# Windowed attention with a feed-forward layer: a refitted planner and a new order of the same work

## The chip, the core and the metric

The kernel runs on one core of a Trainium2 chip. The engines that compute are TensorE (PE: matmuls; PEld is its weight load), VectorE (DVE), ScalarE (ACT) and GpSimd (POOL); SyncE (SP) only issues DMAs. The metric is the device time of one execution in microseconds (us). Before the change the median of 8 runs is 217.38 us, from 216.2 to 218.05.

## What is computed

Attention over 4 batches of 8 heads with 768 positions and 64 values per head; each position sees itself and the 95 before it, and the first 8 positions of its batch ("global"), with a bias by distance. Its output, as 3072 rows of 512, goes through a feed-forward layer: 512 to 2048, h - tanh(h), 2048 to 512.

```python
scores = scale * np.matmul(q, k.transpose(0, 1, 3, 2))
rel = pos[:, None] - pos[None, :]
is_global = pos[None, :] < n_global            # 8
is_local = (rel >= 0) & (rel < n_local)        # 96
dist = np.where(is_global & ~is_local, float(n_local), np.abs(rel))
scores = np.where(is_global | is_local, scores - slopes * dist, -1e9)
a = softmax(scores)
x = (a @ v).transpose(0, 2, 1, 3).reshape(3072, 512)
h = x @ w_in
out = (h - np.tanh(h)) @ w_out
```

## The kernel before

The 3072 rows are 24 tiles of 128, numbered u; six tiles make a batch. A tile's query window reaches into its own 128 keys (o=0) and the 128 before (o=1). Every piece of work has a name, and these names are used from here on:

- `ld kf/qf/vf u` (L211, L216): k, q and v of tile u. The first two tiles' k and q come in fp32 by SP and ACT and are cast (`ck`, `cq`, L238); all else is loaded and cast to bf16 by POOL's DMA queue. `in j`, `out j` (L229): eighths of the two weights, on the same queue.
- `T1 u`, `T u` (L247): for tiles 0 to 7 k and q are transposed on TensorE (L258 with 128 columns, L262 in halves), and `Te u` (L270, L277) copies them out of PSUM. From tile 8 on (`PE_T`) one DMA transpose issued by SP does it (`a_DT`, L264, tile qk).
- `B u` (L282, L149): the bias, put into PSUM by a matmul ahead of the scores, for tiles 0 to 2; `mk` (L156, L149) makes, by the same matmul, the masks that later tiles are multiplied by. Both need the tile dT, which is made on DVE (`distance`, L122) from an iota on POOL and eight scaled identities (`slope`, L142).
- `S u` (L287, L295): scores, transposed; `E u o` (L300): exp on ACT; `M u o` (L305): mask on DVE; `AV u` (L313, L319 and L323): times v, with a row of ones for the sums; `R u` (L327): reciprocal and scaling on DVE, which gives x.
- `X u`, `Xe u` (L342, L354): x transposed on TensorE and copied, for tiles 0 to 8 (`PE_X`); from tile 9 on `Xe u` is a DMA transpose issued by SP (`a_DX`, L357, L358).
- `m1 g f` (L371, L377): x @ w_in for a group g: tiles 0 to 5 singly, then groups of three (m1 7 takes tiles 9, 10 and 11). `th` (L386) and `g` (L390) are tanh on ACT and the subtraction on DVE. `m2 u n` (L402, L409): g @ w_out; `ev` (L414, L419) copies the result out of PSUM and `store` (L421) sends it. The last tile is done in column parts (`parts`, L399).

Nothing here loops in the usual sense. A planner, run when the program is built (`plan`, L585), keeps a model of when each engine, each PSUM bank, each buffer and two DMA rings come free, takes at each step the piece of work that could start earliest, and so writes down one order for each engine. The costs are constants: `op(..., us, ...)` for engines, `T_...` for DMAs, `SLACK_DT` and `SLACK_DX` for how much later than modelled a DMA transpose is assumed to land, `ring` and `share` for the DMA rings, `LOADS` (L433) for the order of the first loads (t: a tile's k, q and v; i: an eighth of w_in; o: of w_out). `NUDGE` shifts the priority of single pieces of work. Each engine then runs its list strictly in order and waits on semaphores; a piece of work whose input is late holds all that stands behind it on that engine.

`with_warm` (L716) fills TensorE's list, up to 14 us of the planner's time, with matmuls of zeros into an unused PSUM bank (`warm`, L368) wherever the plan has a hole. DVE's list begins with the memsets of `ident`, `zero` and eleven tiles of ones (L735 to L738); POOL's with one memset, the identity (L110) and the iotas (L117).

Of the kernel before, what the change touches and what calls it, by code (L numbers as in the profile page):

```python
# [8 lines left out]
BF16 = mybir.dt.bfloat16  # L9
# [6 lines left out]
def kernel(  # L16
# [11 lines left out]
    nc = tc.nc  # L28

    B, H, S, Dh = q.shape  # L30
    P = 128
    NQ = S // P
    NP = H // 2
    NU = B * NQ
# [5 lines left out]
    DM = moe_w_in.shape[0]  # L40
# [10 lines left out]
    PLAIN = 2  # L51
# [14 lines left out]
    cpool = ctx.enter_context(tc.tile_pool(name="const", bufs=1))  # L66
# [17 lines left out]
    slopes = cpool.tile([P, H, P], BF16, name="slopes")  # L84
    xT0 = cpool.tile([P, CD, N0 * P], BF16, name="xT0")
    g0 = cpool.tile([P, CF, N0 * P], BF16, name="g0")
    zero = cpool.tile([P, 512], BF16, name="zero")
    NB = 8
    ps = ps_pool.tile([P, NB, 512], FP32, name="ps")
    banks = {}  # L90
# [75 lines left out]
    ops = {}  # L166
    w_in_r = moe_w_in.rearrange("(c p) f -> p c f", p=P)
    w_out_r = moe_w_out.rearrange("(c p) d -> p c d", p=P)
    PE, ACT, DVE, POOL, SP = ENG.PE, ENG.Activation, ENG.DVE, ENG.Pool, ENG.SP
# [26 lines left out]
    kf, qf, vf = {}, {}, {}  # L196
    kq = {}
# [13 lines left out]
    def load_plain(u, nm):  # L211
        src, dst, eng = {"kf": (k, kf, nc.sync), "qf": (q, qf, nc.scalar)}[nm]
        dst[u] = stpool.tile([P, 2, TJ * Dh], FP32, name=nm)
        started(("ld", nm, u), eng.dma_start(out=dst[u], in_=rows_of(src, u)))
# [151 lines left out]
        return b, i * P, n, 512 // n  # L366

    def warm():  # L368
        nc.tensor.matmul(ps[:, NB - 1, :], zero[:, 0:P], zero, start=True, stop=True)  # L369

    def m1(g, f0):  # L371
        b, o, n, m = shape1(g)
# [24 lines left out]
        )  # L397

    def parts(u):  # L399
        return [(0, 256), (256, 384), (384, 512)] if u == NU - 1 else [(0, DM)]  # L400

    def m2(u, n):  # L402
        part, qq = divmod(n, 4)
# [22 lines left out]

    AHEAD = 5.5
    INF = 1.0e9
    NUDGE = {}
    SLACK_DT, SLACK_DX = 5.0, 2.0  # L430
    WARM = (1.3, 14.0)
    T_ROWS, T_LD, T_W, T_ST, T_DT, T_DX = 0.66, 0.95, 1.32, 0.7, 1.75, 0.9
    LOADS = "tttiiiitiitoooiootiooot"  # L433
    first, n_of = [], {"t": 0, "i": 0, "o": 0}
    for c in LOADS + "t" * NU:
        if n_of[c] < (NU if c == "t" else WJ):
# [12 lines left out]
    for it in first:  # L449
        if it[0] != "t":  # L450
            load(it, 0.75, lambda it=it: load_w(it), T_W)
            continue
        u = it[1]
        for nm in ("vf", "kf", "qf") if u == 0 else ("kf", "qf", "vf"):
            key = ("ld", nm, u)
            if u < PLAIN and nm != "vf":
                op(key, SP, 0.0, lambda: None, at={"kf": (4.75, 7.0), "qf": (4.05, 5.45)}[nm][u], pri=-3,
                   take=["kq"] if nm == "kf" else [])
                continue
            after = []  # L460
            if nm == "vf" and u >= NV:
                after += [("AV", u - NV + 1), ("V", (u - NV) // NQ * NQ + NQ - 2)]
            rows = u < ROWS and nm != "vf"
            load(key, 0.7 if rows else 0.88, lambda u=u, nm=nm: load_bf(u, nm), T_ROWS if rows else T_LD,
                 after=after, take=["kq"] if nm == "kf" else [], slack=1.0 if u == PLAIN + 1 else 0.15)

    op(("dT", 0), DVE, 1.2, distance_0, after=[("nums",)], pri=-2)
    op(("dT", 1), DVE, 0.6, distance_1, after=[("nums",), ("issue", ("dT", 0))], pri=-1)
# [10 lines left out]
    for g, us in enumerate(groups):  # L479
        b, o, n, m = shape1(g)  # L480
# [4 lines left out]
    for m in range(3):  # L485
        for a in range(2):
# [3 lines left out]
               free=[("mk", m, a)], pri=1)  # L490

    for u in range(NU):
# [8 lines left out]
        if u < PE_T:  # L501
            t_us = 0.47 if PLAIN <= u < ROWS else 0.24
            apart = u < APART
            for j, r in ((1, rk), (0, rq)):
                prior = [("issue", ("T1", u))] if j == 0 else []
                name = ("T1" if j else "T", u)
# [3 lines left out]
                     lambda eng, u=u, j=j: a_Te(u, j, eng),  # L510
                     after=[("T1" if j and apart else "T", u)] + ([] if apart or j else [("Te", u, 1)]),
                     free=[name] if apart else [] if j else [("T1", u)])
# [5 lines left out]
        if u < BIASED:  # L518
            for o in os:
                op(("B", u, o), PE, 0.44, lambda u=u, o=o: a_B(u, o), pri=1,  # L520
                   after=biased_by + [("dT", 1) if o else None,
                                    ("issue", ("B", u, 0) if o else ("S", u - 1, 0)) if u or o else None],
                   hold=[(("S", u, o), 2)])
                op(("S", u, o), PE, 0.43, lambda u=u, o=o: a_S(u, (o,)),
                   after=te + [("B", u, o), kdep if o else None])
        else:
            op(("S", u, 0), PE, 0.65 if i else 0.43, lambda u=u, os=os: a_S(u, os),
               after=te + [kdep], hold=[(("S", u, o), 2) for o in os])
        for o in os:
            op(("E", u, o), ACT, 0.93, lambda u=u, o=o: a_E(u, o), after=[("S", u, o if u < BIASED else 0)],  # L530
               take=["p%d" % o], free=[("S", u, o)])
            if u >= BIASED:
                op(("M", u, o), DVE, 0.61, lambda u=u, o=o: a_M(u, o),
                   after=[("E", u, o)] + [("mke", mask_of(u, o), a) for a in range(2)])
        pm = "M" if u >= BIASED else "E"
        if 1 <= i < NQ - 1:
# [3 lines left out]
           after=[(pm, u, 0), (pm, u, 1) if i else None, rv, ("V", u - 1) if i >= 2 else None],  # L540
# [5 lines left out]
        if u < PE_X:  # L546
            op(("X", u), PE, 0.23, lambda u=u: a_X(u), after=[("R", u)], hold=[(("X", u), 1)], give=["x"])
            flex(("Xe", u), [(DVE, 0.34), (ACT, 0.5)], lambda eng, u=u: a_Xe(u, eng),
                 after=[("X", u), xdep], take=xtake, free=[("X", u)])
        else:  # L550
            op(("Xe", u), SP, 0.2, lambda u=u: a_DX(u), after=[("R", u), xdep],
               take=xtake, give=["x"], dma=T_DX, slack=SLACK_DX)
    for g, us in enumerate(groups):
        b, o, n, m = shape1(g)
        w = m * n / 1000.0
        end_b = b and us[-1] % HT == (N0 + HT - 1) % HT
        for f in range(0, CF, m):
            op(("m1", g, f), PE, CD * m * (n / 2400.0 + 0.0025), lambda g=g, f=f: m1(g, f),
               after=[("Xe", us[-1]), ("in", (f + m - 1) // FJ)], hold=[(("m1", g, f), 1)], pri=2,
               give=["xT"] if f + m == CF and end_b else [])  # L560
            op(("th", g, f), ACT, 0.1 + 0.82 * w, lambda g=g, f=f: m1_th(g, f), after=[("m1", g, f)],
               take=["th"], pri=2)
            op(("g", g, f), DVE, 0.06 + 1.05 * w, lambda g=g, f=f: m1_g(g, f), after=[("th", g, f)],
               take=["g"] if f == 0 and b else [], give=["th"], free=[("m1", g, f)], pri=2)
    for u in range(NU):
        g = group_of[u]
        m = shape1(g)[3]
        n_u = 4 * len(parts(u))
        for n in range(n_u):
            part, qq = divmod(n, 4)  # L570
            lo, hi = parts(u)[part]
            op(("m2", u, n), PE, 4 * ((hi - lo) / 2400.0 + 0.0025), lambda u=u, n=n: m2(u, n),
               after=[("out", (4 * qq + 3) // FJ), ("g", g, (4 * qq + 3) // m * m)],
               take=["mo"] if u < EARLY2 and qq == 0 else [], hold=[(("m2", u, part), 1)] if qq == 0 else [],
               give=["g"] if n == n_u - 1 and u >= N0 and u % HT == (N0 + HT - 1) % HT else [], pri=2)
        for part in range(len(parts(u))):
            alt = [(DVE, 0.33)] if part else [(ACT, 0.5), (DVE, 0.56)]
            flex(("ev", u, part), alt, lambda eng, u=u, part=part: m2_e(u, part, eng),
                 after=[("m2", u, 4 * part + 3)], take=["ot"] if part == 0 else [],
                 give=["mo"] if u < EARLY2 else [], free=[("m2", u, part)], pri=1)  # L580
            op(("st", u, part), SP if u == NU - 1 else ACT, 0.1 if u == NU - 1 else 0.4, lambda u=u, part=part: store(u, part), after=[("ev", u, part)],
               give=["ot"] if part == len(parts(u)) - 1 else [], dma=T_ST)


    def plan():  # L585
        bufs = {"mo": 3, "kq": KQ, "p0": 3, "p1": 3,
                "x": 3, "xT": 3, "g": 3, "th": 3, "ot": 4}
        avail = {n: [0.0] * c for n, c in bufs.items()}
        free = {PE: WARM[0], ACT: 3.4, DVE: 1.5, POOL: 1.2, SP: 0.7}
        bank = [0.0] * NB  # L590
        bank[NB - 1] = WARM[1]

# [12 lines left out]
            return at, got  # L605

        ring = {SP: [0.0, []], POOL: [5.7, []]}
        share = {SP: 0.35, POOL: 0.65}
        done, start, width = {}, {}, {}
        f1 = f2 = 0.0  # L610
        queues = {}
# [7 lines left out]
        order = []  # L619
        while waiting or any(queues.values()):  # L620
# [11 lines left out]
            for key, n in cand:  # L632
                o = ops[key]
                eng = o["eng"]
                if o["alt"]:
                    eng = min(o["alt"], key=lambda x: free[x[0]] + 0.6 * x[1])[0]
                t = free[eng]
                via = POOL if o["eng"] is POOL else SP
                if o["dma"] and len(ring[via][1]) >= 8:
                    t = max(t, sorted(ring[via][1])[-8])  # L640
                for a in o["after"]:
                    d = start.get(a[1]) if a[0] == "issue" else done.get(a)
                    if d is None:
                        t = None
                        break
                    t = max(t, d)
                if t is None:
                    continue
                if o["hold"]:
# [3 lines left out]
                    t = max(t, w)  # L653
# [14 lines left out]
            o = ops[key]  # L668
            if o["alt"]:
                o["eng"], o["us"] = eng, dict(o["alt"])[eng]  # L670
                o["fn"] = lambda fn=o["fn"], eng=eng: fn(eng)
            end = t + o["us"]
            free[o["eng"]] = end
            start[key] = t
            if o["at"]:
                done[key] = o["at"]
            elif o["dma"]:
                via = POOL if o["eng"] is POOL else SP
                mine, other, part = ring[via], ring[SP if via is POOL else POOL], share[via]
                begin = max(mine[0], end + (1.0 if via is SP else 1.97))  # L680
                both = min(max(0.0, other[0] - begin), o["dma"] / part)
                mine[0] = begin + o["dma"] + both * (1 - part)
                other[0] += both * part
                done[key] = mine[0] + (0.8 if via is SP else 0.45) + o["slack"]
                mine[1].append(done[key])
            else:
                done[key] = end + LAT[o["eng"]]
# [28 lines left out]
    def with_warm(order):  # L716
        pe = sorted(t for t, key in order if ops[key]["eng"] is PE)
        last = WARM[0]
        n = 0
        for t in pe:  # L720
            us = 0.43 if t < 6.0 else 0.22
            while last + us + 0.08 <= min(t, WARM[1]):
                ops["warm", n] = dict(eng=PE, us=us, fn=warm)
                order.append((last, ("warm", n)))
                last += us
                n += 1
            last = max([last] + [t + ops[key]["us"] for u, key in order if u == t and ops[key]["eng"] is PE])
        return sorted(order, key=lambda x: x[0])

    with tc.manual_schedule(engines={PE, ACT, DVE, POOL, SP}):  # L730
        nc.gpsimd.memset(vb[0][:, :, Dh : Dh + 1], 1.0)
        for u in range(PLAIN):
            load_plain(u, "kf")
            load_plain(u, "qf")
        nc.vector.memset(ident, 0.0)  # L735
        nc.vector.memset(zero, 0.0)  # L736
        for i in range(1, NV):
            nc.vector.memset(vb[i][:, :, Dh : Dh + 1], 1.0)  # L738
        for t, key in with_warm(order):
            ops[key]["fn"]()  # L740
# [35 lines left out]
```

The softmax here doesn't subtract the row's maximum and nothing guards it: scores larger than these inputs give would overflow.

## Time and profile before

| what | us |
|---|---|
| median of 8 runs | 217.38 |
| the profiled execution | 217.27 |
| its span, first to last instruction | 215.4 |
| TensorE's first matmul starts (a warm one) | 1.26 |
| `S 0`, the first scores, starts | 8.51 |
| TensorE's last matmul starts | 211.87 |
| the last store lands | 214.27 |

| engine | busy us | share of the span |
|---|---|---|
| PE | 209.6 | 97% |
| DVE | 132.8 | 62% |
| ACT | 126.1 | 59% |
| POOL | 71.9 | 33% |

Lines of the profile name an engine, a line of the kernel (L377) and the tiles written and read. A matmul's own duration overlaps the next one's, so the time that TensorE spends on something is read here from start to start. The chain of waits follows the work that ended last back to the beginning; "issue" in it is time in which the engine waited for nothing that the profile names. The timeline lists instructions by their start, equal ones merged. "To landing" is the time from the issue of a DMA to the moment its last piece arrives. Start and landing of single instructions are taken from the trace.

### The profile page before, as it was taken

How to read it: one execution, taken by the hardware profiler on the slowest of the kernel's cores; microseconds unless marked ns; L12 is line 12 of the kernel's file. 1: busy time of each engine (PE TensorE's matmuls, PEld its weight loads, DVE VectorE, ACT ScalarE, POOL GpSimd, SP SyncE). 2: the span in 40 equal slices, each digit the busy share in tenths (PEclk: the TensorE clock that was granted, in tenths of full speed). 3: DMA queues.
4: the chain of work that ended last, by engine and by line, in shares of the span. 5: the costliest groups of instructions: out<-in, count | busy, mean ns of one | idle time of the engine just before them, and what ended most of it. 6: DMA issues, size and time to landing. Idle time of an engine off the chain costs nothing.

```text
span 215.4 us, 5046 instructions
## 1 busy us (share of the span) xinstructions
PE 209.6 (97%) x2031; PEld 127.5 (59%) x2031; DVE 132.8 (62%) x286; ACT 126.1 (59%) x207; POOL 71.9 (33%) x92
## 2 busy tenths in 40 slices
PE   7999999999999999989999999999999999999993
PEld 2569976975675665535556555555555555555453
DVE  7456866656685998665867755766765744444311
ACT  3777975564476886525778365776476554434310
POOL 8976749797336464400693000000000000000000
PEclk9999999999999999999999999999999999999999
DMA  5999999999999999999999924224142011101112
GB/s 181 170 194 180 194 187 196 161 163 159 170 190 150 170 152 133 182 162 184 174 183 158 143 73 112 61 73 105 30 112 73 15 64 49 42 10 49 49 52 99
DMA packets 103960, 26.95 MB, mean 125 GB/s; under 512 B 92416, under 2 KB 100992, under 8 KB 103936
## 3 DMA queue, kind: packets, MB, share of 16 engines
q0 software_dynamic: 74048, 13.11, 79.9%
q1 hardware_dynamic: 26032, 6.95, 21.0%
q10 hardware_dynamic: 3856, 6.56, 9.8%
q8 instruction: 16, 0.26, 0.5%
q14 instruction: 8, 0.07, 0.1%
HBM read 27.26 MB, written 6.29 MB: 156 GB/s over the span
## 4 chain that ended last, share of the span: by engine, by line
PE 97%; issue 1%; DVE 0%; DVEq 0%
PE ps L377 40%; PE ps L409 39%; PE ps L295 6%; PE ps L319 3%; PE ps L149 2%; PE ps L323 2%; PE ps L369 2%; PE ps L258 2%; PE ps L346 1%; PE ps L262 1%; DVE ot L419 0%; DVE zero L736 0%; DVE ident L735 0%; DVE vb L738 0%; DVEq L419 0%
## 5 line engine op out<-in xcount | busy, mean ns | idle before, releaser
L377 PE MATMUL ps<-xT,w_in_bf 128*128 128x128 bf16 (+1 forms) x768 | 96.4, 273 | 1.2 <-issue 1.2
L409 PE MATMUL ps<-w_out_bf,g 128*128 128x512 bf16 (+2 forms) x416 | 95.3, 363 | 0.0
L394 DVE TENSOR_TENSOR g<-ps,th 128x384 bf16<-128x384 f32 (+1 forms) x120 | 67.9, 581 | 37.5 <-ACT th L388 34.9
L388 ACT ACTIVATE th<-ps 128x384 f32<-128x384 f32 (+1 forms) x120 | 60.7, 515 | 50.8 <-PE ps L377 49.1
L377 PEld LDWEIGHTS <-w_in_bf 128*128 128x128 bf16 x768 | 58.2, 98 | 31.3 <-issue 1.9
L409 PEld LDWEIGHTS <-g 128*128 128x128 bf16 x416 | 37.8, 98 | 32.8
L303 ACT ACTIVATE pd<-ps 128x1024 bf16<-128x1024 f32 x24 | 24.6, 1024 | 10.3 <-PE ps L295 10.3
L226 POOL DMA_DIRECT2D kq<-in_k_dram x20 | 17.9, 897 | 24.8 <-DMA qk<-kq 18.7
L220 POOL DMA_DIRECT2D vb<-in_v_dram x24 | 21.6, 902 | 10.6 <-DMA kq<-in_k_dram 5.3
L303 ACT ACTIVATE po<-ps 128x1024 bf16<-128x1024 f32 x20 | 20.4, 1022 | 0.0
L226 POOL DMA_DIRECT2D kq<-in_q_dram x20 | 17.9, 897 | 3.6 <-DMA vb<-in_v_dram 3.0
L306 DVE TENSOR_TENSOR pd<-pd,mk 128x1024 bf16<-128x1024 bf16 x21 | 14.5, 689 | 7.6 <-ACT pd L303 7.6
L332 DVE TENSOR_TENSOR x<-ps,rden 128x512 bf16<-128x512 f32 x24 | 16.6, 692 | 0.8
L419 ACT COPY ot<-ps 128x512 f32<-128x512 f32 x19 | 11.1, 586 | 8.6 <-PE ps L409 8.6
L295 PEld LDWEIGHTS <-qk 64*128 64x128 bf16 x352 | 9.9, 94 | 8.4 <-issue 7.5
L295 PE MATMUL ps<-qk 64*128 64x128 bf16 x352 | 14.3, 218 | 0.0
L319 PE MATMUL ps<-vb,pd 128*128 128x65 bf16 x192 | 14.1, 193 | 0.0
L319 PEld LDWEIGHTS <-pd 128*128 128x128 bf16 x192 | 12.5, 97 | 2.5 <-issue 0.2
L306 DVE TENSOR_TENSOR po<-po,mk 128x1024 bf16<-128x1024 bf16 x18 | 12.4, 689 | 2.4 <-ACT po L303 2.4
L323 PE MATMUL ps<-vb,po 128*128 128x65 bf16 x160 | 12.4, 193 | 0.0
L323 PEld LDWEIGHTS <-po 128*128 128x128 bf16 x160 | 10.4, 97 | 1.4
L419 DVE COPY ot<-ps 128x512 f32<-128x512 f32 (+2 forms) x7 | 3.8, 539 | 9.1 <-PE ps L409 9.1
(44 smaller groups left out, 86.4 us busy)
## 6 DMA issues: line engine op xcount, KB each, us to landing
out_dram<-ot ACTq DMA_DIRECT2D x23, 256.0 KB, 2.6
vb<-in_v_dram POOLq DMA_DIRECT2D x24, 128.0 KB, 8.2
kq<-in_k_dram POOLq DMA_DIRECT2D x22, 128.0 KB, 8.0
kq<-in_q_dram POOLq DMA_DIRECT2D x22, 128.0 KB, 7.9
w_in_bf<-in_moe_w_in_dram POOLq DMA_DIRECT2D x8, 256.0 KB, 8.1
w_out_bf<-in_moe_w_out_dram POOLq DMA_DIRECT2D x8, 256.0 KB, 8.9
kf<-in_k_dram SPq DMA_DIRECT2D x2, 256.0 KB, 4.8
qf<-in_q_dram ACTq DMA_DIRECT2D x2, 256.0 KB, 3.6
```

The lines of the kernel that those rows point to most:

```text
L220: i = nc.gpsimd.dma_start(out=vb[u % NV][:, :, 0:Dh], in_=by_head)
L226: i = nc.gpsimd.dma_start(out=dst.rearrange("p (h d) -> p h d", d=Dh), in_=by_head)
L295: nc.tensor.matmul(s[:, slot(2 * p + hh), :], qk[u - o][r, 1, p, :], qk[u][r, 0, p, :], start=u >= BIASED, stop=True, skip_group_check=u < ...
L303: nc.scalar.activation(pr[u, o], s, AF.Exp, bias=0.0, scale=scale)
L306: nc.vector.tensor_tensor(out=pr[u, o], in0=pr[u, o], in1=mk[:, :, mask_of(u, o), :], op=ALU.mult)
L319: nc.tensor.matmul(dst, pr[u, 0][:, slot(h), :], vb[u % NV][:, h, :], start=True, stop=last,)
L323: nc.tensor.matmul(dst, pr[u, 1][:, slot(h), :], vb[(u - 1) % NV][:, h, :], start=False, stop=True,)
L332: nc.vector.tensor_tensor(out=xs[u].rearrange("q (a h) d -> q a h d", a=2), in0=t[:, :, :, 0:Dh], in1=rden.to_broadcast([P, 2, H // 2, Dh] ...
L377: nc.tensor.matmul(t[:, (f - f0) * n : (f - f0 + 1) * n], w_in_bf[j][:, c, fo : fo + P], xT[b][:, c, o : o + n], start=(c == 0), stop=(c = ...
L388: nc.scalar.activation(h_view(ths[g, f0], g), h_view(hs[g, f0], g), AF.Tanh, bias=0.0, scale=1.0)
L394: nc.vector.tensor_tensor(out=gs[b][:, f0 : f0 + m, o : o + n], in0=h_view(hs.pop((g, f0)), g), in1=h_view(ths.pop((g, f0)), g), op=ALU.su ...
L409: nc.tensor.matmul(os_[u, part][:, 0 : hi - lo], gs[b][:, f, t * P : (t + 1) * P], w_out_bf[f // FJ][:, f % FJ, lo:hi], start=(f == 0), st ...
```

## The change

The planner gets new constants: TensorE's work counts double up to `COLD`, a delay stands for a fetch of instructions in the DMA ring, the slacks of DMA transposes go from 5 and 2 to 4 and 4, the rings share evenly, and eight pieces of work get a nudge. Out of this comes another order on all engines. Two things are edited by hand: the zero tile is 128 columns wide instead of 512 (its matmul reads it four times over) and is set before `ident`; and the last tile's column parts are 256, 192 and 64 instead of 256, 128 and 128.

```diff
--- before.py
+++ after.py
@@ -84,7 +84,7 @@
     slopes = cpool.tile([P, H, P], BF16, name="slopes")
     xT0 = cpool.tile([P, CD, N0 * P], BF16, name="xT0")
     g0 = cpool.tile([P, CF, N0 * P], BF16, name="g0")
-    zero = cpool.tile([P, 512], BF16, name="zero")
+    zero = cpool.tile([P, P], BF16, name="zero")
     NB = 8
     ps = ps_pool.tile([P, NB, 512], FP32, name="ps")
     banks = {}
@@ -366,7 +366,10 @@
         return b, i * P, n, 512 // n
 
     def warm():
-        nc.tensor.matmul(ps[:, NB - 1, :], zero[:, 0:P], zero, start=True, stop=True)
+        nc.tensor.matmul(
+            ps[:, NB - 1, :].rearrange("p (a f) -> p a f", f=P), zero,
+            zero.unsqueeze(1).to_broadcast([P, 4, P]), start=True, stop=True,
+        )
 
     def m1(g, f0):
         b, o, n, m = shape1(g)
@@ -397,7 +400,7 @@
         )
 
     def parts(u):
-        return [(0, 256), (256, 384), (384, 512)] if u == NU - 1 else [(0, DM)]
+        return [(0, 256), (256, 448), (448, 512)] if u == NU - 1 else [(0, DM)]
 
     def m2(u, n):
         part, qq = divmod(n, 4)
@@ -426,11 +429,22 @@
 
     AHEAD = 5.5
     INF = 1.0e9
-    NUDGE = {}
-    SLACK_DT, SLACK_DX = 5.0, 2.0
-    WARM = (1.3, 14.0)
+    NUDGE = {
+        ('E', 11, 0): 0.6,
+        ('R', 3): -0.3,
+        ('Te', 7, 0): 0.15,
+        ('m1', 3, 0): -0.6,
+        ('m1', 5, 4): -0.6,
+        ('m1', 6, 10): -0.3,
+        ('th', 5, 0): 1.0,
+        ('th', 6, 10): -0.6,
+    }
+    SLACK_DT, SLACK_DX = 4.0, 4.0
+    WARM = (1.1, 14.0)
+    COLD = 6.3
+    FETCH = (15.8, 0.9)
     T_ROWS, T_LD, T_W, T_ST, T_DT, T_DX = 0.66, 0.95, 1.32, 0.7, 1.75, 0.9
-    LOADS = "tttiiiitiitoooiootiooot"
+    LOADS = "tttitiiiiiootoiotoiooot"
     first, n_of = [], {"t": 0, "i": 0, "o": 0}
     for c in LOADS + "t" * NU:
         if n_of[c] < (NU if c == "t" else WJ):
@@ -462,7 +476,7 @@
                 after += [("AV", u - NV + 1), ("V", (u - NV) // NQ * NQ + NQ - 2)]
             rows = u < ROWS and nm != "vf"
             load(key, 0.7 if rows else 0.88, lambda u=u, nm=nm: load_bf(u, nm), T_ROWS if rows else T_LD,
-                 after=after, take=["kq"] if nm == "kf" else [], slack=1.0 if u == PLAIN + 1 else 0.15)
+                 after=after, take=["kq"] if nm == "kf" else [], slack=0.15)
 
     op(("dT", 0), DVE, 1.2, distance_0, after=[("nums",)], pri=-2)
     op(("dT", 1), DVE, 0.6, distance_1, after=[("nums",), ("issue", ("dT", 0))], pri=-1)
@@ -574,7 +588,7 @@
                take=["mo"] if u < EARLY2 and qq == 0 else [], hold=[(("m2", u, part), 1)] if qq == 0 else [],
                give=["g"] if n == n_u - 1 and u >= N0 and u % HT == (N0 + HT - 1) % HT else [], pri=2)
         for part in range(len(parts(u))):
-            alt = [(DVE, 0.33)] if part else [(ACT, 0.5), (DVE, 0.56)]
+            alt = [(DVE, 0.3)] if part else [(ACT, 0.5), (DVE, 0.56)]
             flex(("ev", u, part), alt, lambda eng, u=u, part=part: m2_e(u, part, eng),
                  after=[("m2", u, 4 * part + 3)], take=["ot"] if part == 0 else [],
                  give=["mo"] if u < EARLY2 else [], free=[("m2", u, part)], pri=1)
@@ -586,7 +600,7 @@
         bufs = {"mo": 3, "kq": KQ, "p0": 3, "p1": 3,
                 "x": 3, "xT": 3, "g": 3, "th": 3, "ot": 4}
         avail = {n: [0.0] * c for n, c in bufs.items()}
-        free = {PE: WARM[0], ACT: 3.4, DVE: 1.5, POOL: 1.2, SP: 0.7}
+        free = {PE: WARM[0], ACT: 3.4, DVE: 1.5, POOL: 1.0, SP: 0.7}
         bank = [0.0] * NB
         bank[NB - 1] = WARM[1]
 
@@ -605,7 +619,7 @@
             return at, got
 
         ring = {SP: [0.0, []], POOL: [5.7, []]}
-        share = {SP: 0.35, POOL: 0.65}
+        share = {SP: 0.5, POOL: 0.5}
         done, start, width = {}, {}, {}
         f1 = f2 = 0.0
         queues = {}
@@ -669,7 +683,7 @@
             if o["alt"]:
                 o["eng"], o["us"] = eng, dict(o["alt"])[eng]
                 o["fn"] = lambda fn=o["fn"], eng=eng: fn(eng)
-            end = t + o["us"]
+            end = t + o["us"] * (2.0 if o["eng"] is PE and t < COLD else 1.0)
             free[o["eng"]] = end
             start[key] = t
             if o["at"]:
@@ -680,6 +694,8 @@
                 begin = max(mine[0], end + (1.0 if via is SP else 1.97))
                 both = min(max(0.0, other[0] - begin), o["dma"] / part)
                 mine[0] = begin + o["dma"] + both * (1 - part)
+                if begin < FETCH[0] <= mine[0]:
+                    mine[0] += FETCH[1]
                 other[0] += both * part
                 done[key] = mine[0] + (0.8 if via is SP else 0.45) + o["slack"]
                 mine[1].append(done[key])
@@ -718,13 +734,13 @@
         last = WARM[0]
         n = 0
         for t in pe:
-            us = 0.43 if t < 6.0 else 0.22
+            us = 0.43 if t < COLD else 0.22
             while last + us + 0.08 <= min(t, WARM[1]):
                 ops["warm", n] = dict(eng=PE, us=us, fn=warm)
                 order.append((last, ("warm", n)))
                 last += us
                 n += 1
-            last = max([last] + [t + ops[key]["us"] for u, key in order if u == t and ops[key]["eng"] is PE])
+            last = max([last] + [t + ops[key]["us"] * (2 if t < COLD else 1) for u, key in order if u == t and ops[key]["eng"] is PE])
         return sorted(order, key=lambda x: x[0])
 
     with tc.manual_schedule(engines={PE, ACT, DVE, POOL, SP}):
@@ -732,8 +748,8 @@
         for u in range(PLAIN):
             load_plain(u, "kf")
             load_plain(u, "qf")
+        nc.vector.memset(zero, 0.0)
         nc.vector.memset(ident, 0.0)
-        nc.vector.memset(zero, 0.0)
         for i in range(1, NV):
             nc.vector.memset(vb[i][:, :, Dh : Dh + 1], 1.0)
         for t, key in with_warm(order):
```

What that does to the lists, read from the two programs as built. TensorE's list has the same matmuls but for the warm ones, 7 instead of 11 (six ahead of `B 0`, as before, and one ahead of `S 0` instead of five). Its beginning:

```
before: warm x6, B 0, mk x4,             T1 0, T 0,       warm x5, S 0, B 1 0, T1 1, T 1,        T1 2, AV 0, T 2, S 1 0, ...
after:  warm x6, B 0, mk x2, T1 0, T 0,  mk x2,           warm,    S 0,        T1 1, T 1, B 1 0, T1 2, AV 0, T 2, S 1 0, ...
```

Between the tiles 9 and 14 and the group that needs 9, 10 and 11:

```
before: S 11, m2 5 3, S 12, m1 6 14, m2 6 0, m1 6 15, AV 11, m2 6 1, AV 12, m2 6 2, S 13, m2 6 3, m2 7 0-1, S 14, AV 13, m2 7 2-3, m2 8 0-1, AV 14, m2 8 2, m1 7
after:  S 11, m1 6 12, m2 5 2, m1 6 13, m2 5 3, S 12, m1 6 14, AV 11, m2 6 0, m1 6 15, m2 6 1, AV 12, m2 6 2, S 13, m2 6 3, m2 7 0-2, AV 13, S 14, m2 7 3, m2 8 0-1, m1 7, AV 14
```

SP's list (T: transpose of q and k, Xe: transpose of x):

```
before: T8 T9 T10 T11 T12 Xe9 T13 T14 Xe10 Xe12 Xe11 Xe13 T15 Xe14 T16 T17 T18 Xe15 Xe16 T19 Xe17 Xe18 T20 T21 Xe19 Xe20 T22 Xe21 T23 Xe22 Xe23
after:  T8 T9 T10 T11 Xe9 T12 T13 Xe10 T14 Xe11 Xe12 Xe13 T15 T16 Xe14 T17 Xe15 T18 Xe16 T19 Xe17 T20 Xe18 T21 Xe19 T22 Xe20 Xe21 T23 Xe22 Xe23
```

On ACT, `Te 0` (q) now stands before the masks of `mk 2`, not after the first of them. Of the 26 copies of results ACT does 16 instead of 19 and DVE 10 instead of 7; of the nine copies of x ACT does 3 instead of 1 and DVE 6 instead of 8.

## The prediction

> **What bounds the kernel now.** I read the busy shares first, then the chain, then the timeline of both ends and of every place where TensorE stood still.
>
> ```profile
> PE 209.6 (97%) x2031; PEld 127.5 (59%) x2031; DVE 132.8 (62%) x286; ACT 126.1 (59%) x207; POOL 71.9 (33%) x92
> PE 97%; issue 1%; DVE 0%; DVEq 0%
> ```
>
> TensorE is the bound and the other engines are a third idle. But "97% busy" holds warm matmuls, which do no work, and matmuls at the slow clock. So the question is where TensorE loses time, and the chain in order of time tells that:
>
> ```profile
> 1.26 2.74 PE ps L369 x6
> 4.01 2.58 PE ps L149 x6
> 6.59 0.90 PE ps L258 x8
> 7.49 1.08 PE ps L369 x5
> ...
> 96.14 1.21 issue
> 97.34 9.26 PE ps L377 x56
> ```
>
> Two losses are seen: eleven warm matmuls (L369) around the six of bias and masks (L149), and one hole before L377, which is m1 7. From start to start the hole is 1.37 us: the m2 part before it starts at 95.11 and ends its fourth step at 95.97, and m1 7 starts at 97.34. Between 8.51 and 211.87 nothing else on TensorE is longer than the 0.1 us that a change of matmul kind takes. So all that can be won lies before 8.51, at 96, and behind 211.87.
>
> **The start.** Before:
>
> ```profile
> 1.26 2.74 PE L369 MATMUL ps<-zero 128*128 128x512 bf16 x6 [1.26 <-DVE vb L738]
> 3.85 2.74 PE L149 MATMUL ps<-slopes,dT 128*128 128x512 bf16 x6
> 6.38 1.11 PE L258 MATMUL ps<-ident,kq 128*128 128x128 bf16 x8
> 7.31 1.26 PE L369 MATMUL ps<-zero 128*128 128x512 bf16 x5
> 7.53 0.59 ACT L277 COPY qk<-ps 128x512 bf16<-128x512 bf16 x1 [0.61 <-PE ps L258]
> 8.51 0.40 PE L295 MATMUL ps<-qk 64*128 64x128 bf16 x8
> ```
>
> A 512-column matmul steps by 0.427 us up to 6.38 and by 0.216 from 7.55 on: the trace's clock record opens at 6.49. The eight transposes of tile 0 (L258) step by 0.116 on both sides of the opening (0.118 for the one issued before it), and those of tile 1, at 9.4, by 0.116 too. So these transposes cost the same at either clock and are the right work for the slow one; mk is not.
>
> After, step by step. `zero` is set first and in 0.11 us instead of 0.27 (the memset of 64 words, `ident`, takes 0.11): the first warm starts about 1.0, 0.26 earlier, which only lengthens the pause behind the six, to 0.4 us. `ident` comes 0.11 later, and with it POOL's identity, the eight slopes and dT: B 0 at 3.95 instead of 3.85 (+0.1). It and two masks are four steps of 0.427: T1 0 at 5.66; its cast is done at 5.40, as before, so it doesn't wait. From T1 0 to the end of the copy that S 0 needs, before took 6.38 to 8.12, 1.74; with 0.06 to hand over, S 0 at 7.46. What TensorE has until then fits: transposes to 6.59, two masks and a warm at 0.216 to 7.24. ACT is free at 6.5 for the copy, since mk 2 now stands behind it. Gain so far 1.05 us.
>
> Part is given back at once. S 0 (0.33), T1 1, T 1 and B 1 (0.44 to 0.46 each) bring T1 2 to 9.13, but k of tile 2 landed at 9.33 and POOL's queue starts 0.11 later: 9.44, and T1 2 at 9.50. Before it was 10.29, so **0.79** stays. Bounds: 1.05 if the load comes earlier, 0.3 if each later load or chain in the first 40 us is as tight.
>
> I followed the rest of the start by the same rows. AV 1 needs both exps of tile 1; ACT's list (masks, E 0, two copies, two exps at 1.03) ends at 13.70, TensorE gets there at 13.68. The loads change places: tile 3 moves ahead of in 1 to in 3. With the spacings of before (0.67 for a row load, 0.95 for v, 1.34 for a weight), in 1 lands at 15.9 and in 3 at 18.7, and m1 0 wants them at 16.2 and 19.4. Weight in 7 is wanted 1.5 us later than before, at 38.1, against a landing at 35.7.
>
> **The rest of TensorE's list.** I added the median steps of before, kind by kind, in both orders from S 0 to the last matmul: 201.61 and 201.64 us. The same work, so the order itself costs nothing; only waits can.
>
> **The hole at 96.** m1 7 needs the transposed x of tiles 9, 10 and 11.
>
> ```profile
> 80.70 13.03 SPq L358 DMA_TRANSPOSE xT<-x  x4
> 87.26 2.52 SPq L358 DMA_TRANSPOSE xT<-x  x2
> 97.34 1.46 PE L377 MATMUL ps<-xT,w_in_bf 128*128 128x384 bf16 x8 [1.21 <-issue]
> ```
>
> The two that start at 87.26 are Xe 12 and, behind it, Xe 11. x of tile 11 was ready at 85.93, but SP waited for x of tile 12 (87.23) and issued Xe 11 at 88.50; it landed at 97.26, 0.09 before m1 7. In the new list Xe 11 stands ahead. By the rows AV 11 to m1 7 is now 11.8 us of TensorE work (10 parts of m2 at 0.863, one of m1 at 0.65, three AV, two S); x is ready 1.62 after AV 11's start, so 10.2 us are left to land. Xe 9 to Xe 14 took 6.64 to 9.03 us from issue to landing. The hole goes, **1.37**, with 1.1 to 3.5 to spare.
>
> What is late next? Three transposes of q and k. S 9 moves to 62.9 and T 9, whose place in the queues is unchanged, lands at 61.3: 1.6 to spare where it was 5.9. T 12 is now queued behind Xe 9, which waits for AV 9: 1.62 for x and 1.19 for its issue, so T 12 is issued near 69.6 instead of 66.98, and so are the loads that wait for its kq buffer. From AV 9 to S 12 is 14.05 us, which leaves T 12 11.2. T 8 to T 15 took 8.10 to 12.23, median 9.6: from 3.1 to spare to 1.0 short. I take none, as six of the eight lie under 10.
>
> **The end.** TensorE's time is equal: 16 steps of 192 columns (0.082, by width) and 16 of 64 (0.029, the row of 65 columns in L319) are 1.78 us, as two times 16 at 0.056. The last copy shrinks from 128 to 64 columns:
>
> ```profile
> 211.23 0.29 DVE L419 COPY ot<-ps 128x128 f32<-128x128 f32 x1 [0.47 <-PE ps L409]
> 212.19 0.29 DVE L419 COPY ot<-ps 128x128 f32<-128x128 f32 x1 [0.67 <-PE ps L409]
> ```
>
> 256 columns took 0.42, so 64 take 0.23: **0.06** gained. The wider copy before it ends at 212.1, in time for SP. The last store took 1.76 us for 64 KB and the 128 KB one 1.73, so half the size saves nothing; pieces of 256 bytes instead of 512 could cost some, from nothing to 0.1 by the same two rows. The copies moved between ACT and DVE cost nothing: both are under 63% busy.
>
> **Sum.** 0.79 + 1.37 + 0.06 = 2.2 us off the profiled execution's 217.27: 215.1. It is 0.11 under the median, which I neglect.
>
> **A rule against it.** The row: in before the clock opened after 5.2 us of 512-column matmuls with no pause above 0.05; after has a pause of 0.4 and transposes from 5.66 on. The Trainium skill ("TensorE: Matmul & The Clock Gate", section "Part 4: PE-mode transpose") says that transposes do not count as PE-busy in the same way; its section "What's actually happening" gives windows of 3.4 us that run freely. By both, one missed window would put the opening at 9.9, the masks, S 0 and B 1 would run slow, and by an estimate 0.6 us of the 2.2 would go; by the row alone nothing goes. I go by the row, since once open the clock stayed open from 8.5 to 15.4 amid transposes.
>
> **Rivals.**
> 1. *The wait moves to a transpose of q and k.* T 12 at the longest row (12.23) holds S 12 by 1.0, and its lag is passed on in SP's queue to T 13 and Xe 10. For it: T 9 and T 10 took 12.23 and 11.52. Against: those were issued while loads ran at full rate. 216.1 to 216.5.
> 2. *The start is hidden*, because loads come no sooner: 0.79 falls to nothing, 215.8 to 216.0. Against: the slacks above.
> 3. *The hole stays*: Xe 11 lands no sooner, as the DMA engines are full whatever the order; its landing after Xe 12's was 3.4 us. 216.5.
> 4. *Slower: the clock stays slow until the dense m1 at 16.* Place: T 0 to m1 0. Price: 0.21 for each 512-column matmul (two masks, B 1 and B 2 with eight), about 0.2 for each of five S, 0.24 and 0.48 for AV 0 and AV 1, 0.22 for each X, less the 0.37 that T1 2 would have waited: 4.0, so 219.1. It is slower by over 0.5% if the clock opens after about 14.5. For: the pause and the transposes. Against: 4.3 of the 5.5 us before 6.5 are full matmuls still.
>
> **Chances.** Forecast 0.55; rival 1 0.17, rival 2 0.14, rival 3 0.08, rival 4 0.06. Half of rival 1 and most of rival 2 lie more than 0.5% under before, about what a measurement of this kernel can tell from no change: faster 0.72, same 0.22, slower 0.06. The range takes in the full 1.05 at the start and some tenths of an earlier clock (214.3), and rivals 1 to 3 (216.9).
>
> **What would show it.** S 0 near 7.5 and T1 2 near 9.5 with its wait ended by kq's load; one warm matmul instead of five ahead of S 0; no "issue" before m1 7, at about 93.6; S 9 and S 12 without idle time ahead; the last copy at 0.23. A 512-column step of 0.427 after 7 would show the clock's rival; TensorE idle at S 12 the first. I am wrong if a new hole over 1 us stands anywhere between 16 and 211.

## The result and the profile after

The changed kernel takes 215.06 us (median of 11 runs, 214.62 to 215.99) against 216.96 for the kernel before (32 runs): a ratio of 0.9916, 95% interval 0.99 to 0.9933. The profiled execution took 215.21 with a span of 213.4; the span is 1.9 us shorter. The forecast was 215.1.

From the page of the changed kernel, busy shares and chain:

```profile
PE 208.3 (98%) x2027; PEld 127.4 (60%) x2027; DVE 133.2 (62%) x287; ACT 125.1 (59%) x206; POOL 71.9 (34%) x92
PE 94%; DMA 2%; DVE 1%; ACT 0%; ACTq 0%; issue 0%; DVEq 0%
```

TensorE has four matmuls less (the warm ones) and "issue", which was the hole, is gone from the chain. New in it are 2% of DMA and 1% of DVE: the chain now begins with a load, not with warm matmuls. The timeline of the start shows which (start, duration, engine, line; in brackets the idle time before it and what ended that):

```profile
0.99 2.74 PE L369 MATMUL ps<-zero 128*128 128x512 bf16 x6 [0.99 <-DVE zero L751]
3.24 0.17 DVE L134 TENSOR_SCALAR dT<-dT 128x8 bf16<-128x8 bf16 x1
3.53 1.91 PE L149 MATMUL ps<-slopes,dT 128*128 128x512 bf16 x4
5.23 1.11 PE L258 MATMUL ps<-ident,kq 128*128 128x128 bf16 x8
6.46 0.71 DVE L239 CAST kq<-qf 128x512 bf16<-128x512 f32 x1 [1.34 <-DMA qf<-in_q_dram]
7.10 0.67 DVE L277 COPY qk<-ps 128x512 bf16<-128x512 bf16 x1
7.82 0.40 PE L295 MATMUL ps<-qk 64*128 64x128 bf16 x8 [0.83 <-DVE qk L277]
...
11.69 1.03 ACT L303 ACTIVATE pd<-ps 128x1024 bf16<-128x1024 f32 x1
12.19 0.40 PE L295 MATMUL ps<-qk 64*128 64x128 bf16 x8
12.77 1.02 PE L149 MATMUL ps<-slopes,dT 128*128 128x512 bf16 x4 [0.18 <-ACT pd L303]
```

B 0 starts at 3.53, earlier than both the old 3.85 and the forecast 3.95; tile 0's transposes end early; but the copy that S 0 needs stands on DVE behind the cast of tile 1's q, and that waits for a load that landed at 6.44. So S 0 starts at 7.82, 0.69 earlier than before. At 12.37 there is a second wait: B 2 takes over the PSUM banks of S 1 0, and ACT's exp is done reading them only at 12.72. The step from the last matmul of S 1 0 to B 2 is 0.40 us; in e10 below, where nothing is waited for, it is 0.15, so the wait is 0.25. From T1 2 (9.61, was 10.29) to S 8 (60.19, was 60.56) the gain shrinks from 0.68 to 0.37. No other step on TensorE behind S 0 is longer than 0.31.

The hole, in the timeline of SP and of TensorE:

```profile
84.01 9.29 SPq L358 DMA_TRANSPOSE xT<-x  x3
...
94.19 0.81 PE L380 MATMUL ps<-xT,w_in_bf 128*128 128x384 bf16 x4
```

The first of the three is Xe 11, at 84.01 straight after its x was ready (83.98); it landed at 90.84, 3.3 us ahead of m1 7, which starts without idle time. From S 8 to TensorE's last matmul it is 149.90 us instead of 151.31, so 1.41 is won there, about the size of the hole. The last copy is as small as forecast (groups by shape: mean ns after the bar):

```profile
L422 DVE COPY ot<-ps 128x192 f32<-128x192 f32 x1 | 0.4, 358 | 0.8 <-PE ps L412 0.8
L422 DVE COPY ot<-ps 128x64 f32<-128x64 f32 x1 | 0.2, 225 | 0.1
```

### The profile page after: what moved, and what is told of

Its sections match the earlier page's. It is cut to its first block, busy times and chain, and to the rows that moved or that the text cites. A ratio compares the mean times of both kernels' runs of the same rounds, so it can differ in the third digit from the quotient of the medians.

```text
span 213.4 us, 5037 instructions
## 1 busy us (share of the span) xinstructions
PE 208.3 (98%) x2027; PEld 127.4 (60%) x2027; DVE 133.2 (62%) x287; ACT 125.1 (59%) x206; POOL 71.9 (34%) x92
## 4 chain that ended last, share of the span: by engine, by line
PE 94%; DMA 2%; DVE 1%; ACT 0%; ACTq 0%; issue 0%; DVEq 0%
PE ps L380 40%; PE ps L412 39%; PE ps L295 6%; PE ps L319 3%; DMA qf<-in_q_dram 2%; PE ps L323 2%; PE ps L258 1%; PE ps L346 1%; PE ps L149 1%; PE ps L262 1%; ACT pd L303 0%; ACTq L214 0%; DVE kq L239 0%; DVE x L332 0%; DVE qk L277 0%
## 5 line engine op out<-in xcount | busy, mean ns | idle before, releaser
L412 PE MATMUL ps<-w_out_bf,g 128*128 128x512 bf16 (+3 forms) x416 | 94.8, 363 | 0.0
L306 DVE TENSOR_TENSOR pd<-pd,mk 128x1024 bf16<-128x1024 bf16 x21 | 14.5, 688 | 8.6 <-ACT pd L303 8.4
L422 ACT COPY ot<-ps 128x512 f32<-128x512 f32 x16 | 9.4, 586 | 7.6 <-PE ps L412 7.6
L422 DVE COPY ot<-ps 128x512 f32<-128x512 f32 (+3 forms) x10 | 5.8, 585 | 10.9 <-PE ps L412 10.8
```

The costliest lines, as they stand in the source:

```text
L306: nc.vector.tensor_tensor(out=pr[u, o], in0=pr[u, o], in1=mk[:, :, mask_of(u, o), :], op=ALU.mult)
L412: nc.tensor.matmul(os_[u, part][:, 0 : hi - lo], gs[b][:, f, t * P : (t + 1) * P], w_out_bf[f // FJ][:, f % FJ, lo:hi], start=(f == 0), st ...
```

## The experiments

My theory after the result: the hole at 96 is the larger part, caused by SP's order; the start gives some tenths; the column parts next to nothing; and the rest of the new order nothing. Rivals: the new order as a whole brings the gain; or the start's part is the luck of an early clock. The edits below lie in the list of work just before it is emitted (`keys`), so nothing is planned anew. All ratios are against executions of the kernel before that were made beside it.

**e1, e5: the order of two transposes.** In the kernel before Xe 11 is put ahead of Xe 12; in the changed kernel, behind it.

```diff
+        keys.remove(('Xe', 11))
+        keys.insert(keys.index(('Xe', 12)), ('Xe', 11))
```

> The kernel before, with one swap in SP's list: the transpose of x of tile 11 ahead of that of tile 12. Theory (the hole ahead of m1 7 is SP's order): Xe 11 is issued near 86.0 instead of 88.5, lands by 95, the 1.37 us hole goes, and with a median of before of 217.0 the time is 215.6. Rival (the DMA engines are full whatever the order, so Xe 11 lands near 97 anyway): 217.0, the hole stays. Rival (the gain of the change comes from the new order as a whole): 0.3 or less is won here.

Measured: 215.46, ratio 0.993 (0.9912 to 0.9948), 1.5 us less. Timelines of SP and TensorE in e1:

```profile
80.20 13.10 SPq L358 DMA_TRANSPOSE xT<-x  x4
...
95.47 0.81 PE L377 MATMUL ps<-xT,w_in_bf 128*128 128x384 bf16 x4
```

Xe 11 was issued at 85.46 and landed at 92.55; m1 7 follows at 95.47 with no idle time. The DMA engines were not the limit. From S 8 to the last matmul it is 149.93 us here, against 149.90 in the changed kernel: with this one exchange the old order is as short as the new one over that stretch.

> The changed kernel with Xe 12 put ahead of Xe 11 again, the one thing undone. Theory: Xe 11 is issued near 87.8 instead of 84.0, and lands near 94.7 to 95.0 instead of 90.8, past the 94.2 at which m1 7 would start: a hole of 0.5 to 0.8, 215.6 to 215.9. Not the whole 1.37 returns, as the new order of TensorE asks for m1 7 0.4 to 0.8 us later after AV 11. Rival (the order of these two isn't the cause): 215.1.

Measured: 216.81, ratio 0.9994 (0.9975 to 1.0013). With two neighbours exchanged nearly the whole gain is gone, more than I expected:

```profile
86.17 6.65 SPq L358 DMA_TRANSPOSE xT<-x  x3
...
94.81 0.81 PE L380 MATMUL ps<-xT,w_in_bf 128*128 128x384 bf16 x4 [0.92 <-DVE po L306]
```

Xe 12 goes out at 86.17, Xe 11 behind it at 87.42 and lands at 94.72; m1 7 stands still for 1.09 us by its steps. (DVE is named, as the landing is not matched to a line; the trace has it 0.09 before the start.) TensorE reached m1 7 at 93.7 here, 0.5 us earlier than in the changed kernel's profile (S 0 was at 7.33), so the hole is larger than the 0.5 to 0.8 that I had counted. The ratios differ by 1.7 us; where the rest lies isn't settled.

**e2, e9: the start.** e2 is the kernel before with the new start, e9 the changed kernel with the old one. The diff of e2 (the zero tile as in the change, besides):

```diff
+        for n in range(7, 11):
+            keys.remove(("warm", n))
+        move(("mk", 2, 0), ("T", 0))
+        move(("mk", 2, 1), ("mk", 2, 0))
+        move(("mke", 2, 0), ("Te", 0, 0))
```

> The kernel before with the start of the change alone: zero tile of 128 columns set first, masks of mk 2 behind the transposes of tile 0, one warm matmul instead of five ahead of S 0. Theory: S 0 starts at 7.4 to 7.9 instead of 8.51, of which some is lost again by 60 us as in the changed kernel (0.69 at S 0, 0.37 at S 8); the hole ahead of m1 7 stays at 1.3 to 1.4; 0.4 to 0.7 less, 216.3 to 216.6. Rival (the start is hidden by the loads): 217.0. Rival (the clock opens later because of the transposes): 512-column steps of 0.427 past 6.5 and 217.0 or more.

Measured: 215.88, ratio 0.9963 (0.9939 to 0.9987), about 0.8 us less by the ratio; the median lies under the forecast 216.3 to 216.6. S 0 started at 7.06. The hole was not 1.3 in this profile but 0.05: Xe 11 took 7.4 us to land, not 8.75. In e12 below the hole was 1.13, and Xe 11 took 8.51. So the hole's size changes from run to run with that one DMA; why it does isn't settled. How much of the 0.8 is the start and how much a smaller hole can't be told.

> The changed kernel with the old start: zero tile of 512 columns set behind ident, masks of mk 2 ahead of the transposes of tile 0 (with the PSUM banks that they had), five warm matmuls ahead of S 0; all else as changed. Theory: B 0 at 3.85 instead of 3.53, S 0 at 8.0 to 8.5, and 0.3 to 0.6 more, 215.4 to 215.7. Rival (the start is hidden by the loads, which come at the same time): 215.1. Rival (the start as predicted, 0.79): 215.9.

Measured: 215.68, ratio 0.9941 (0.9922 to 0.996); S 0 at 8.51, T1 2 at 10.29, as in the kernel before to the hundredth. Against the changed kernel's 0.9916 the new start is worth about 0.5 us, between "hidden" and the 0.79 of the prediction; the intervals overlap. e9 keeps the rest of the new order, B 1 behind the transposes of tile 1 included.

**e3: three edits by hand.** e2's start, e1's swap and the column parts, in the old order.

> The kernel before with the swap of Xe 11 and Xe 12, the start, and the column parts 256, 192 and 64: three edits by hand, all else in the old order and with the old constants. Theory (the three make up the gain, the rest of the new order is worth nothing): 1.4 + 0.4 + 0.15 less, 215.0, the changed kernel's 215.1. Rival (loads and tiles in the new order carry part of it): 215.6 or more.

Measured: 214.93, ratio 0.9922 (0.9894 to 0.995). The old order with these edits is as fast as the changed kernel, so no gain was found that needs the new constants, loads or tile order. The interval leaves room for some tenths.

**e6, e7: warm matmuls.** The changed kernel with five instead of one ahead of S 0 (e6), and with none at all (e7, the second diff).

```diff
+        for n in range(7, 11):
+            ops["warm", n] = ops["warm", 6]
+            keys.insert(keys.index(("S", 0, 0)), ("warm", n))
```

```diff
+        keys = [key for key in keys if key[0] != "warm"]
```

> The changed kernel with four more warm matmuls ahead of S 0, so that five stand there as before. Theory (in the new order TensorE waits there for DVE's copy of k anyway: from 6.62 to 7.82 in the profile of the changed kernel): four times 0.216 end by 7.7, so nothing is lost where the copy is as late as that, and up to 0.3 where q of tile 1 lands early; 215.1 to 215.4. Rival (every warm matmul taken away is time won): 0.86 more, 215.9.

Measured: 215.41, ratio 0.9936 (0.9912 to 0.996), about 0.4 more than the changed kernel, between the two forecasts; the intervals overlap. In this profile the casts were early, the five warm matmuls ran from 6.94 to 8.0 and held S 0 until 8.12, against 7.0 to 7.4 in the other profiles of the new start, the changed kernel's 7.82 apart. So the room for them that I read from the changed kernel's profile is not there as a rule. S 8 stood at 60.32, against 60.19 in the changed kernel's profile and 59.72 in that of e5, which has the same start: single profiles do not tell how much of the price is left there.

> The changed kernel without any warm matmul: TensorE starts with B 0 at 3.53. In the profiles so far the clock opened 3.3 to 5.2 us after TensorE's first matmul. Theory (transposes count for it as other matmuls do): it opens at 6.8 to 8.7; the masks are slow (0.4) but end before DVE's copy; 0 to 0.6 more, 215.1 to 215.7. Rival (transposes don't count as busy, and the pause of the prediction's rival is fatal): it opens at 10 or later, and 1 to 4 us are lost.

Measured: 215.25, ratio 0.9929 (0.9905 to 0.9954). The clock opened at 9.48, 6.0 us after TensorE's first matmul; that is later than I had said, but with warm matmuls e9 and e10 had 5.7 and 5.8. No loss can be told from the changed kernel. Its timeline:

```profile
3.47 1.89 PE L149 MATMUL ps<-slopes,dT 128*128 128x512 bf16 x4 [3.47 <-DVE dT L134]
5.28 1.08 PE L258 MATMUL ps<-ident,kq 128*128 128x128 bf16 x8
6.18 1.03 PE L149 MATMUL ps<-slopes,dT 128*128 128x512 bf16 x2
7.14 0.61 PE L295 MATMUL ps<-qk 64*128 64x128 bf16 x8
8.60 1.02 PE L149 MATMUL ps<-slopes,dT 128*128 128x512 bf16 x2
9.55 0.63 PE L262 MATMUL ps<-ident,kq 128*64 128x128 bf16 x8
```

The 512-column pairs take 1.02 instead of 0.61, and the scores 0.61 instead of 0.40, but most of what stands between is transposes, which take the same 1.1 at either clock (0.116 a step, in e7 ahead of the opening as in e1 behind it), and T1 2 at 9.55 is where it was in the changed kernel (9.61).

**e8, e10, e11: what holds the new start.** e8 puts DVE's copy of tile 0's k ahead of the cast of tile 1's q; e10 gives three pieces of work other PSUM banks (the second diff); e11 does both.

```diff
+        keys.remove(("cq", 1))
+        keys.insert(keys.index(("Te", 0, 1)) + 1, ("cq", 1))
```

```diff
+        banks.update({("S", 1, 1): 6, ("S", 2, 0): 4, ("AV", 1): 2})
```

> The changed kernel with one swap on DVE: the copy of tile 0's transposed k ahead of the cast of tile 1's q, which waits for a load that landed between 5.4 and 6.46. Theory (that cast holds S 0): S 0 at 7.0 to 7.1 in every run, T1 2 at 9.2 to 9.4 as k of tile 2 lands near 9.1; 0.1 to 0.4 less, 214.7 to 215.0. Rival (what is won at S 0 is taken back by B 2's wait for a PSUM bank at 12.4, or by loads): 215.1.

Measured: 214.94, ratio 0.9912 (0.9891 to 0.9933), which can't be told from the changed kernel. S 0 was at 7.34, since tile 0's own cast ended late in this profile (5.53), and the next cast then held T1 1. The load of tile 1's q landed at 5.4 to 5.8 us in all the other profiles; the 6.44 of the changed kernel's was an exception, and the wait that I blamed is short as a rule.

> The changed kernel with other PSUM banks for three pieces of work: S 1 1 in 6 and 7, S 2 0 in 4 and 5, AV 1 in 2 and 3. In every profile of the changed order so far B 2 0 waits 0.37 us at 12.4 for ACT's exp of tile 1, whose banks it takes over. Theory (that wait is the planner's choice of bank and takes back half of what the start has won): the step at 12.4 falls from 0.40 to 0.15, S 8 comes 0.2 to 0.37 earlier, 214.7 to 214.9. Rival (behind it AV 1 waits for the second exp of tile 1, or the loads hold m1 0): the wait moves, 215.1.

Measured: 214.42, ratio 0.99 (0.9881 to 0.992). The two bias blocks of tile 2 in its timeline, right behind the scores:

```profile
11.57 0.40 PE L295 MATMUL ps<-qk 64*128 64x128 bf16 x8
11.90 1.04 PE L149 MATMUL ps<-slopes,dT 128*128 128x512 bf16 x4
12.01 1.02 ACT L303 ACTIVATE po<-ps 128x1024 bf16<-128x1024 f32 x1
```

There is no wait, and S 8 starts at 59.18.

> The changed kernel with both: the other banks, and DVE's copy of tile 0 ahead of the cast of tile 1's q. Theory (the two waits lie one behind the other): 0.4 to 0.6 less than the changed kernel, 214.5 to 214.7, and S 8 near 59.5. Rival (the exps on ACT between S 1 and AV 1 are the next bound): 214.9, as with the copy alone.

Measured: 214.99, ratio 0.9918 (0.9902 to 0.9934). Here k of tile 2 landed at 9.66 instead of 8.5 to 9.4, and T1 2 waited 0.56 for it; why its load was late isn't settled, and the two edits together weren't shown to help.

> The kernel with the other banks once more, as its first interval (0.9881 to 0.992) overlaps that of the changed kernel (0.99 to 0.9933). Theory (the 0.37 us wait at B 2 is gone for good): 0.990 again, 214.4 to 214.7 against a before of 217.0. Rival (its first runs were lucky in the loads: T1 2 stood at 8.99 in that profile and at 9.61 in the changed kernel's): 0.9915.

Measured: 214.41, ratio 0.9897 (0.9855 to 0.9939); S 8 at 59.14. By the ratios this kernel takes 0.35 and 0.4 us less than the changed one, and the wait is gone in both profiles; the intervals of the ratios still overlap. The rival about the loads isn't ruled out: T1 2, which the three banks do not touch, stood early again (8.95). From T1 2 to S 8, behind that, it is 50.19 us in both profiles of this kernel and 50.29 in e11, against 50.58 in the changed kernel; that part goes with the banks. It is the fastest version found.

**e12: the zero tile alone**, in the kernel before.

> The kernel before with only the zero tile changed (128 columns, set first). Theory (B 0 comes earlier because DVE's small tensor_scalar on dT, 0.56 us in each profile with the old memsets and 0.17 in each with the new, no longer ends with POOL's second DMA issue): B 0 at 3.53 instead of 3.85, and, as DVE's casts and the five warm matmuls stay, 0 to 0.3 less: 216.7 to 217.0. Rival (the prediction's: ident comes 0.1 later and B 0 with it): 3.95 and 217.1.

Measured: 216.79, ratio 0.9991 (0.9973 to 1.0009). B 0 stood at 3.53, so the edit to the zero tile is what brings it forward, and nothing that can be measured was won by it: five warm matmuls still stood behind it, and the hole (1.13 in this profile) too.

## Why the prediction came out, step by step

- **The hole** was right in cause and size: 1.37 forecast, 1.41 between the two profiles, 1.5 by e1, 1.7 between e5 and the changed kernel. It was a matter of two neighbours in SP's list. Xe 11 had 3.3 us to spare, at the upper end of the 1.1 to 3.5.
- **The start** was probably mis-sized: 0.79 forecast; 0.68 at T1 2 in the profile, 0.37 left at S 8, about 0.5 by e9, 0.8 by e2 with a smaller hole in it, 0.2 from e1 to e3 with the column parts in it. The intervals are wider than these differences. Whatever the size, three terms were wrong. "`ident` comes 0.11 later, and with it B 0 at 3.95" failed, as dT came 0.38 earlier. "From T1 0 to the end of the copy 1.74" failed, as I had looked at the copy on ACT and not at what stands ahead of the other one on DVE. And "only waits can" cost anything was followed for loads and exps but not for PSUM banks, where the 0.25 at B 2 was. T1 2 came at 9.61 for a forecast 9.50, but not because of k's load, which had landed at 9.11.
- **The fixed clock** was a hidden assumption. The start was worked out from a profile whose clock opened at 6.49. e1 has the same start to the instruction, its clock opened at 5.40, and S 0 stood at 8.00 instead of 8.51. In e12, with TensorE's old list, the clock opened at 4.18, S 8 stood at 59.73 for 60.56 before, and no gain could be measured over its executions. So half a microsecond and more of any comparison of two single profiles here can be the clock, and the 0.37 at S 8 is such a comparison. The profiles alone don't rule out that the start's part is the luck of an early clock; against it stand e2's ratio over 12 executions, whose interval ends at 0.9987, and less clearly e9's.
- **The transposes of q and k** did not become late: S 9 had 3.7 us to spare and S 12 2.8 (1.6 forecast for each). T 12 was issued at 70.48, behind Xe 9, as forecast, and took 8.14.
- **The end**: the copy took 0.225 us for a forecast 0.23. The time from the last matmul's start to the end of the span went from 3.49 to 3.35, but lies between 3.29 and 4.16 over all profiles with either parts, so the 0.06 can't be seen.
- **The rule against it** did not decide. The pause of 0.4 that it and rival 4 start from did not come: as dT was early, B 0 followed the sixth warm matmul by one step of 0.427. In the changed kernel the clock opened at 5.58, among the transposes. In e7, where only eight 512-column matmuls, some transposes and the first scores came before it, it opened 6.0 us after the first matmul, at the upper end of the spread of all profiles. Whether transposes count less can't be told from that; they did not keep the clock shut in these runs. Rival 4, which needs it shut past 14.5, has no run for it.

So the sum came out near the truth (2.2 forecast, 1.9 by the medians) by one term that was right and one that was probably too large. In the two profiles the 1.92 is 0.37 up to S 8, 1.41 from there to the last matmul and 0.14 behind it. That the time itself was met to 0.04 us is in part luck: 2.2 was taken off an execution of 217.27, and the median of the kernel before came out at 216.96, from which the same sum would have given 214.8.

## What to carry to other kernels

When the bound engine is full, look in its trace for the few places where it stands still, and follow each back through the queue of whoever issued the input: here one issue that waited behind a neighbour was worth more than all other new priorities. Work that costs the same at the slow clock, as these transposes do, is a candidate for the first microseconds; that exchange was not run by itself. Warm matmuls were worth nothing that could be measured. A planner's choice of PSUM bank is a wait like any other, and is found by asking of each late matmul who last read its banks.

## What the runs showed of the hardware

The clock opened between 2.8 and 6.0 us after TensorE's first matmul in the 14 profiles (2.8 in e13, 3.3 in e3, 5.2 in before, 5.8 in e10, 6.0 in e7). The Trainium skill ("TensorE: Matmul & The Clock Gate", section "What's actually happening") has a window of 3.4 us that runs freely; the spread of 3.0 us over the 13 profiles that begin with the same six warm matmuls (2.8 to 5.8) agrees with that, its "±500ns" doesn't.

DVE's tensor_scalar on 128x8 elements took 0.56 to 0.57 us in the three profiles with the old memsets (before, e1, e9) and 0.17 in the eleven with the new, where POOL's DMA issues stand 0.12 later. In the kernel before:

```profile
1.90 1.90 POOL L220 DMA_DIRECT2D vb<-in_v_dram  x2
...
3.23 0.56 DVE L134 TENSOR_SCALAR dT<-dT 128x8 bf16<-128x8 bf16 x1
```

It ended at 3.79, when POOL's second DMA issue ended (2.91 to 3.80). The Trainium skill ("SBUF — State Buffer", section "SBUF: two separate sides") says that DVE, for some of its instructions, and GpSimd share a pair of ports and that the one who comes second is blocked for the whole instruction. These rows look like that, but those of the changed kernel do not:

```profile
2.02 1.90 POOL L220 DMA_DIRECT2D vb<-in_v_dram  x2
```

There the second issue ran from 3.03 to 3.92, the tensor_scalar at 3.24 lay within it too, and it took 0.17. So the cause of the 0.56 stays open.
